# Five plain pairs and three seven-product pairs instead of six and two in the first pass of a retention and softplus-FFN kernel

## The chip, the cores and the metric

The kernel runs on one core of a Trainium2 chip. The metric is the device time of one execution in microseconds (us); lower is better. The core has five engines that run their own instruction streams and wait for each other through semaphores: PE (matrix products; its weight loads are shown as PEld), DVE (elementwise work), ACT (activations and copies), POOL (slower elementwise work) and SP, which here only issues DMAs.

## The reference, cut to what matters

```python
scores = scale * q @ k.T                     # per batch (8), head (8): 576 x 64
ret = scores * Dmat                          # decay gamma ** (i - j), lower triangle
x = (ret @ v).transpose(...).reshape(4608, 512)
h = x @ w_in                                 # 512 -> 2048
g = np.maximum(h, 0.0) + np.log1p(np.exp(-np.abs(h)))
return g @ w_out                             # 2048 -> 512, float32
```

A retention (attention with a decay instead of a softmax) gives 4608 tokens of 512 values; a two-layer network with a softplus between follows.

## The kernel before

All products have float32 accuracy. A value is split into a head and a rest, and a product is three matmuls (`TERMS`: rest by head, head by rest, head by head). One matmul has a 128x128 weight tile and 512 columns.

The tokens are cut into 9 units of 512. Unit 0 is computed while the weights are prepared. Units 1 and 2 form one "super unit", which this change is about; units 3 to 8 follow in three more (`full_pair`, `full_phase`). The hidden layer has 16 slices of 128, that is 8 pairs J = 0 to 7. For a pair of hidden slices and a pair of units, the 2x2 block product can be done in two ways:

- **plain** (`plain_slot`, one call for each slice p and each unit u): two block products of 6 matmuls each, so 48 matmuls for a pair over both units;
- **seven products** (`strassen_pair`, line 1022): 7 block products, 42 matmuls, and additions on DVE and ACT. It gives both units at once; the results of unit 2 are stored in `kept_dram` and fetched again at the end of the pass over unit 2 (`kept_parts`).

`PLAIN = 6` (line 56) sets how many pairs are plain. The order on all engines is the order in which the code is written: first 12 plain slots of unit 1 (p = 0 to 11), then the seven-product pairs J = 6 and 7, then 12 plain slots of unit 2, then the four kept slices of J = 6 and 7, then `full_pair`.

In a plain slot PE does the two block products into a PSUM bank (`acc` or `third`, in turn), then perhaps an attention group, then 12 output matmuls (line 504) of an earlier slice. `outputs` is a queue: slices are appended at the end of a slot and 12 matmuls are taken off in each. At the start of unit 2 the queue holds two slices of the seven-product pairs, so **in unit 2 the output matmuls of slice p run in slot p + 2**. An attention group (`chunk_products`, 13 of them in both units) is 48 to 64 small matmuls into the banks `two` and `third`; DVE then reads `third` in `states_out` (lines 272, 273, 282), masks scores (244) and scales values (430). The next product that writes `third` waits for these reads. In unit 2 the groups stand in slots with odd p, and the slot behind uses `third`.

Around this, DVE, ACT and POOL prepare things for later, by tables (`schedule`) that name a slot for each step:

- sums of blocks of the first-layer weights (`prepare_*`) and of the second-layer weights (`whole_in`, `combine_out`, `split_out`, `store_out`), stored to DRAM for the later products. `whole_in(j, at)` adds head and rest of the output weights 2j and 2j+1 (line 652) and **writes the sums into the buffers of the output weights 2at and 2at+1**, tags `w{p}`, in place of what stood there;
- combinations of the activations for units 3 and 4: `start_combined(i)` on POOL (lines 448 to 451), `finish_combined(i)` (ACT 455, DVE 456), `half_x` (ACT 435, DVE 438).

All DMAs are issued by SP, in the order written. Weight blocks come through a ring of 7 buffers, each reloaded after a product (`block_load`). `queued` is a list of DMAs that are issued one or two after each product (`queued_some`), `behind` one that is appended to `queued` later. Scratch tiles of 4 KB a partition come from a pool of 9 (`quad`).

Of the kernel before, what the change touches and what calls it, by code (L numbers as in the profile page):

```python
# [55 lines left out]
PLAIN = 6  # L56
# [28 lines left out]
def retention_softplus_ffn(ctx: ExitStack, tc, first, whole, others, consts, w, out):  # L85
# [440 lines left out]
    def output_out(u, tt, last=0):  # L526

        y = ys[u][tt]
        if u not in places:
            places[u] = [quad() for _ in range(2)]  # L530
        osb = places[u][tt // 2][:, tt % 2]
        if tt % 2 == last:
            nc.scalar.copy(osb, y)
        else:
            nc.vector.tensor_copy(osb, y)
        r = u * T + tt * P
        if u < 2:
            nc.sync.dma_start(out[r:r + P, :], osb)
        else:
            behind.append(lambda: nc.sync.dma_start(out[r:r + P, :], osb))  # L540
# [126 lines left out]
    def combine_head(f):  # L667
        for a in f:
            nc.scalar.copy(a[:, HI].bitcast(F32R), a[:, LO])
# [286 lines left out]
    def prepare_rest(j):  # L956
        combine_rest(raws[j])
# [4 lines left out]
    def raw_store(j):  # L962
        for p, n in ((2 * j, 2 * P), (2 * j + 1, 4 * P)):
            nc.sync.dma_start(wout_dram[p][:, :, 0:n].bitcast(F32), wouts[p][:, :, 0:n].bitcast(F32))
# [32 lines left out]
    def half_b22(i):  # L997
# [8 lines left out]
        (6, prepare_ring, 4, 0, 3, 2), (7, prepare_store, PLAIN + 1), (7, prepare_ring, 4, 3, 4, 3),  # L1006
        (7, finish_combined, 1, nc.vector), (7, half_b22, 2), (8, prepare_sums, 4), (9, prepare_ring, 5),
        (9, finish_combined, 2, nc.vector), (10, prepare_split, 4), (10, prepare_sums, 5), (10, half_b22, 3),
        (11, prepare_store, 4), (11, finish_combined, 3, nc.vector), (11, prepare_head, 5),
        (0, whole_out, 0), (1, combine_out, 0), (2, split_out, 0), (3, store_out, 0),  # L1010
        *[(5 + 2 * j, raw_store, j) for j in range(4)])
    starts = schedule(*[(3 + 2 * i, start_combined, i) for i in range(CPU)])
    for p in range(2 * PLAIN):
        group = groups.pop() if p % 2 == 0 and p < 10 else None
        plain_slot(1, p, B11, B21, rest, group, (), *(x.get(p, ()) for x in (jobs, starts)))
# [6 lines left out]
    def strassen_pair(s, J, group, rest, last=False, extra=None):  # L1022
# [14 lines left out]
        for j in stores:  # L1037
            prepare_rest(j)
# [27 lines left out]
        if extra is not None:  # L1066
            combine_head(raws["out", extra])
        ab4 = softplus_of(c[3])
        queued_some(len(queued))
        if group:  # L1070
            chunk_products(*group, None)
            coming_steps = next_steps(group[0]) if s == 0 and J == NJ - 1 else []
            group_out(*group)
            if extra is not None:
                combine_rest(raws["out", extra])
            for k in coming_steps:
                scale_values(k)
# [14 lines left out]
    stores = [5]  # L1092

# [6 lines left out]
    extras = {(0, NJ - 2): 1, (0, NJ - 1): 2}  # L1100
    for s in range(FULL):
# [3 lines left out]
        for J in range(first, NJ):  # L1105
            rest, kept = strassen_pair(s, J, groups.pop() if groups else None, rest, s == 0 and J == NJ - 1,
                                       extras.get((s, J)))
# [10 lines left out]
        if first:  # L1118
            blocks = schedule((0, prepare_ring, 0))
            plan = schedule(  # L1120
                *[(2 * j - 1, prepare_ring, j) for j in range(1, 4)], *[(2 * j, prepare_sums, j) for j in range(4)],
                *[(2 * j + 1, prepare_split, j) for j in range(4)], *[(2 * j + 2, prepare_store, j) for j in range(4)],
                *[(8 + 2 * i, finish_combined, i, nc.vector) for i in range(2)],
                (9, half_x, B21, STAGE[1, 0], whole, nc.vector), *[(2 * j - 7, raw_store, j) for j in range(4, NJ)],
                (4, whole_in, 3, 0), (6, combine_out, 3), (7, split_out, 3), (8, store_out, 3),
                (8, whole_in, 4, 1), (9, combine_out, 4), (10, split_out, 4), (11, store_out, 4))
            starts = schedule(*[(min(6 + 2 * i, 2 * first - 1), start_combined, i) for i in range(CPU)])
            for p in range(2 * first):
                group = groups.pop() if p % 2 else None
                if p == 0:  # L1130
                    while stores:
                        prepare_rest(stores[0])
                        prepare_store(stores.pop(0))
                if p == 2 * first - 1:
                    kept += [fetch(first)]
                plain_slot(u2, p, B12, B22, rest, group, *(x.get(p, ()) for x in (blocks, plan, starts)))
                rest = []
            job((0, 0), finish_combined, 2, nc.vector)
            job((0, 1), half_x, B11, STAGE[0, 0], whole, nc.vector)
            job((1, 0), finish_combined, 3, nc.vector)  # L1140
            job((1, 1), half_x, B22, STAGE[1, 1], whole, nc.vector)
        else:
# [5 lines left out]
        for n, J in enumerate(range(first, NJ)):  # L1148
# [5 lines left out]
            while stores:  # L1154
                prepare_rest(stores[0])
                prepare_store(stores.pop(0))
# [281 lines left out]
```

## Time and profile before

| | |
|---|---|
| three runs | 820.05, 820.60, 820.61 us; median 820.6 |
| profiled execution | 820.36 us, its span 818.6 us |
| busy time | PE 810.1 us (99%), DVE 572.4 (70%), ACT 394.7 (48%), POOL 135.4 (17%) |
| granted TensorE clock | 0.999 of full speed |
| DMA | 209.92 MB, 256 GB/s mean |
| unit 1 and the seven-product pairs | 115 to 227 us of the span |
| unit 2, plain | 227 to 303 us |
| kept slices and the first `full_pair` | 303 to 332 us |

The span runs from the first to the last instruction; 1.76 us of the profiled execution lie around it. Matmul ends are modelled in the trace, so matmuls are read by their starts.

### The profile page before, as it was taken

To read this page: it belongs to the slowest core of one execution; us is meant where nothing else is said; L and a number is where in the kernel's file an instruction comes from. 1 tells how busy PE (TensorE), PEld (TensorE's weight loads), DVE (VectorE), ACT (ScalarE), POOL (GpSimd) and SP (SyncE) were. 2 spreads that over 40 slices of the span, in tenths; PEclk is the share of its full clock that TensorE was granted. 3 is DMA by queue.
4 is the path that set the end of the run, shared out by engine and by line. 5 is a ranking of instruction groups with operands and counts; after the bars stand their busy time and mean duration, and the time that the engine had idled before them with its cause. 6 is when DMAs were issued, how large, how long until landed. Compare 5 with 4: busy or idle time off the path is not lost.

```text
span 818.6 us, 18782 instructions
## 1 busy us (share of the span) xinstructions
PE 810.1 (99%) x7369; PEld 664.9 (81%) x7369; DVE 572.4 (70%) x962; ACT 394.7 (48%) x698; POOL 135.4 (17%) x208
## 2 busy tenths in 40 slices
PE   8999999999999999999999999999999999999998
PEld 6778878888888888888888888888888888888886
DVE  5999976776676784756869984656769944345785
ACT  6778763324522434534354564334355644434543
POOL 4322221541121453112111000111100000000000
PEclk9999999999999999999999999999999999999999
DMA  9998879887889985698888778778757676666665
GB/s 360 322 314 288 314 241 370 292 293 254 283 307 346 329 281 171 200 318 261 276 260 298 219 222 253 255 234 262 221 170 222 216 242 199 194 195 192 201 212 172
DMA packets 149399, 209.92 MB, mean 256 GB/s; under 512 B 10816, under 2 KB 115008, under 8 KB 149312
## 3 DMA queue, kind: packets, MB, share of 16 engines
q1 hardware_dynamic: 149312, 208.72, 77.4%
q8 instruction: 59, 0.97, 0.5%
q14 instruction: 28, 0.23, 0.1%
HBM read 166.74 MB, written 41.94 MB: 255 GB/s over the span
## 4 chain that ended last, share of the span: by engine, by line
PE 97%; DMA 1%; DVE 0%; SPq 0%; issue 0%; ACT 0%; DVEq 0%
PE acc L891 21%; PE sum L1183 20%; PE y L504 16%; PE third L891 12%; PE h L465 5%; PE two L891 5%; PE two L1183 4%; PE third L226 2%; PE third L1183 2%; PE acc L1183 2%; PE two L210 2%; PE two L288 2%; PE two L300 1%; DMA raw<-whole 1%; PE bank L210 0%
## 5 line engine op out<-in xcount | busy, mean ns | idle before, releaser
L891 PE MATMUL acc<-xt,ring 128*128 128x512 f32 x768 | 193.3, 389 | 0.1
L1183 PE MATMUL sum<-parts,ring 128*128 128x512 f32 (+1 forms) x723 | 173.7, 391 | 0.0
L891 PEld LDWEIGHTS acc<-xt,ring 128*128 128x128 f32 x768 | 143.9, 188 | 30.8 <-DVE quad L1056 0.5
L1183 PEld LDWEIGHTS sum<-parts,ring 128*128 128x128 f32 x723 | 134.2, 188 | 28.2
L1177 DVE TENSOR_TENSOR parts<-g,parts 128x512 fp32r<-128x512 f32 x168 | 113.5, 692 | 52.8 <-ACT parts L1173 51.7
L504 PE MATMUL y<-wout,g 128*128 128x512 f32 x576 | 141.0, 393 | 0.0
L1173 ACT CAST parts<-g 128x512 fp32r<-128x512 f32 x168 | 103.8, 622 | 68.5 <-PE sum L1183 25.3
L504 PEld LDWEIGHTS y<-wout,g 128*128 128x128 f32 x576 | 106.6, 188 | 24.2 <-DVE g L497 1.7
L891 PE MATMUL third<-xt,ring 128*128 128x512 f32 x444 | 110.9, 389 | 0.0
L891 PEld LDWEIGHTS third<-xt,ring 128*128 128x128 f32 x444 | 83.4, 188 | 17.3
L488 ACT ACTIVATE g<-g 128x512 f32<-128x512 f32 x96 | 59.0, 631 | 78.4 <-DVE g L1205 36.2
L203 POOL TENSOR_TENSOR qv<-qv,consts_sb 128x256 f32<-128x256 f32 x61 | 43.0, 705 | 132.8 <-DMA qv<-others 129.3
L1205 DVE TENSOR_TENSOR g<-two,g 128x512 f32<-128x512 f32 x24 | 16.6, 692 | 54.2 <-PE two L891 51.8
L497 DVE TENSOR_TENSOR g<-ab,g 128x512 fp32r<-128x512 f32 x44 | 31.6, 718 | 27.4 <-ACT g L493 26.7
L465 PE MATMUL h<-xt,win 128*128 128x512 f32 x192 | 47.8, 397 | 1.5 <-ACT xt L414 1.5
L493 ACT CAST g<-ab 128x512 fp32r<-128x512 f32 x44 | 27.3, 621 | 44.5 <-PE y L504 40.6
L1203 ACT COPY g<-acc 128x512 f32<-128x512 f32 x24 | 14.1, 588 | 68.7 <-PE acc L891 68.7
L465 PEld LDWEIGHTS h<-xt,win 128*128 128x128 f32 x192 | 35.1, 188 | 10.0 <-ACT xt L414 2.2
L891 PE MATMUL two<-xt,ring 128*128 128x512 f32 x168 | 42.6, 390 | 0.0
L284 POOL TENSOR_TENSOR s<-s,consts_sb 128x256 f32<-128x256 f32 (+1 forms) x31 | 20.7, 667 | 106.7 <-DVE s L282 95.7
L891 PEld LDWEIGHTS two<-xt,ring 128*128 128x128 f32 x168 | 31.4, 188 | 6.8 <-DVE xs L430 0.3
L226 PEld LDWEIGHTS third<-qv,keys 64*64 64x64 f32 x776 | 27.0, 134 | 9.0 <-issue 8.6
(186 smaller groups left out, 1199.7 us busy)
## 6 DMA issues: line engine op xcount, KB each, us to landing
ring<-split SPq DMA_DIRECT2D x126, 256.0 KB, 4.5
ring<-combined SPq DMA_DIRECT2D x104, 256.0 KB, 3.6
ring<-outcombined SPq DMA_DIRECT2D x96, 256.0 KB, 3.4
qv<-others SPq DMA_DIRECT2D x61, 320.0 KB, 4.7
ring<-outsplit SPq DMA_DIRECT2D x72, 256.0 KB, 3.5
wst<-w SPq DMA_DIRECT2D x32, 512.0 KB, 5.8
keys<-others SPq DMA_DIRECT2D x61, 256.0 KB, 4.9
split<-win SPq DMA_DIRECT2D x16, 512.0 KB, 6.0
```

Of the source, the lines that this page charges most:

```text
L203: nc.gpsimd.tensor_mul(v, v, f.unsqueeze(2).broadcast_to([P, 4, D]))
L226: return nc.tensor.matmul(L["T"][rows[h], t, part[s]], L["kp"][rows[t], s, rows[h]], L["v"][rows[t], s, rows[h]], start=True, stop=True, s ...
L284: nc.gpsimd.tensor_mul(s, s, f.unsqueeze(2).broadcast_to([P, 2 * n, D]))
L465: nc.tensor.matmul(h, wins[p][:, a, kt * P:(kt + 1) * P], xt[:, b, T1 + kt // 2, kt % 2], start=(n == 0), stop=(n == 3 * NKT - 1))
L488: nc.scalar.activation(out, h, AF.Softplus)
L493: nc.scalar.copy(g[:, HI], ab)
L497: nc.vector.tensor_sub(g[:, LO], ab, g[:, HI].bitcast(F32))
L504: nc.tensor.matmul(ys[u][tt], g[:, a, tt * P:(tt + 1) * P], wouts[p][:, b], start=(p == 0 and n == 0), stop=(p == NF - 1 and n == 2))
L891: nc.tensor.matmul(bank, w[:, ta, kt * P:(kt + 1) * P], xt[:, tb, x, kt], start=start and k == 0, stop=k == 5, skip_group_check=True)
L1173: nc.scalar.copy(t[:, HI], g_slot(J, n))
L1177: nc.vector.tensor_sub(t[:, LO], g_slot(J, n), t[:, HI].bitcast(F32))
L1183: nc.tensor.matmul(bank[m][:, at], w[:, a, m * P:(m + 1) * P], t[:, b, at], start=start and n == 0, stop=n == 2, skip_group_check=True)
```

## The change

`PLAIN` becomes 5: unit 1 has 10 plain slots, then the seven-product pairs J = 5, 6, 7, then 10 plain slots of unit 2 and six kept slices. The number of attention groups stays 13: five in the plain slots of unit 1, three (before: two) in seven-product pairs, five (before: six) in unit 2. The tables are rewritten for the shorter passes. The first-layer sums of pair 7 are now made inside the seven-product pair J = 5, for use in J = 7. The stores of unit 0's and 1's outputs and of the second-layer weights go through `queued`.

```diff
-PLAIN = 6
+PLAIN = 5
@@ output_out
-        if u < 2:
-            nc.sync.dma_start(out[r:r + P, :], osb)
-        else:
-            behind.append(lambda: nc.sync.dma_start(out[r:r + P, :], osb))
+        (queued if u < 2 else behind).append(lambda: nc.sync.dma_start(out[r:r + P, :], osb))
@@ raw_store
-            nc.sync.dma_start(wout_dram[p][:, :, 0:n].bitcast(F32), wouts[p][:, :, 0:n].bitcast(F32))
+            queued.append(lambda p=p, n=n: nc.sync.dma_start(wout_dram[p][:, :, 0:n].bitcast(F32),
+                                                             wouts[p][:, :, 0:n].bitcast(F32)))
@@ unit 1's slots
-        group = groups.pop() if p % 2 == 0 and p < 10 else None
+        group = groups.pop() if p % 2 == 0 else None
@@ strassen_pair
-    def strassen_pair(s, J, group, rest, last=False, extra=None):
+    def strassen_pair(s, J, group, rest, last=False, extra=None, more=None):
...
-        for j in stores:
-            prepare_rest(j)
+        if more is not None:
+            prepare_whole(more)
+            prepare_sums(more)
...
+        if more is not None:
+            prepare_head(more)
+            if more + 1 < NJ:
+                prepare(more + 1)
...
+            if more is not None:
+                prepare_rest(more)
+                stores.append(more)
...
+    late_sums = {PLAIN: PLAIN + 2}
@@ unit 2's table, the rows of the second-layer sums
-                (4, whole_in, 3, 0), (6, combine_out, 3), (7, split_out, 3), (8, store_out, 3),
-                (8, whole_in, 4, 1), (9, combine_out, 4), (10, split_out, 4), (11, store_out, 4))
-            starts = schedule(*[(min(6 + 2 * i, 2 * first - 1), start_combined, i) for i in range(CPU)])
+                (2, whole_in, 3, 0), (4, combine_out, 3), (6, split_out, 3), (7, store_out, 3), (8, whole_in, 4, 3))
+            starts = schedule(*[(min(4 + 2 * i, 2 * first - 1), start_combined, i) for i in range(CPU)])
```

Three places show what moves. Names: `wout3_182` is output weight 3 and so on, `sums_` the tile that `whole_in` writes (its first tile takes the first buffer named by `at`, its second tile the second), `u`, `sx`, `s` what `states_out` makes, `y0` to `y3` the four output banks.

DVE in unit 2, around `whole_in(3, 0)`. Before, it stands in slot 4:

```order
L497 TENSOR_TENSOR g_3399<-ab_3397,g_3399 128x512
L662 TENSOR_TENSOR quad_3369<-quad_3370 128x256
L663 TENSOR_TENSOR quad_3369<-quad_3369 128x256
L664 TENSOR_TENSOR quad_3370<-quad_3369 128x256
L665 TENSOR_TENSOR quad_3370<-quad_3369,quad_3370 128x256
L652 TENSOR_TENSOR sums_3420<-wout6_185 128x512
L652 TENSOR_TENSOR sums_3421<-wout7_972 128x512
L272 TENSOR_TENSOR u_3509<-third_1738,s_3346 128x256
L273 TENSOR_TENSOR sx_3508<-third_1738,s_3346 64x256
```

Now, in slot 2:

```order
L497 TENSOR_TENSOR g_3328<-ab_3326,g_3328 128x512
L659 TENSOR_TENSOR quad_3298<-quad_3299 128x256
L660 TENSOR_TENSOR quad_3298<-quad_3298 128x256
L661 TENSOR_TENSOR quad_3299<-quad_3298 128x256
L662 TENSOR_TENSOR quad_3299<-quad_3298,quad_3299 128x256
L649 TENSOR_TENSOR sums_3353<-wout6_185 128x512
L649 TENSOR_TENSOR sums_3354<-wout7_972 128x512
L272 TENSOR_TENSOR u_3444<-third_1738,s_3269 128x256
L273 TENSOR_TENSOR sx_3443<-third_1738,s_3269 64x256
```

The rows read alike, two slots earlier: the two additions write the buffers of output weights 0 and 1, and behind them stand the state steps of the next slot's group.

PE right behind that group. Before (slot 5):

```order
L300 MATMUL two_1736<-qv_3154,sx_3341 64x64
L504 MATMUL y0_3227<-wout3_182,g_3349 128x512 x3
L504 MATMUL y1_3228<-wout3_182,g_3349 128x512 x3
L504 MATMUL y2_3229<-wout3_182,g_3349 128x512 x3
L504 MATMUL y3_3230<-wout3_182,g_3349 128x512 x3
L891 MATMUL third_1738<-xt_186,ring_3220 128x512 x6
L891 MATMUL third_1738<-xt_186,ring_3255 128x512 x6
```

Now (slot 3):

```order
L300 MATMUL two_1736<-qv_3101,sx_3264 64x64
L504 MATMUL y0_3331<-wout1_180,g_3272 128x512 x3
L504 MATMUL y1_3332<-wout1_180,g_3272 128x512 x3
L504 MATMUL y2_3333<-wout1_180,g_3272 128x512 x3
L504 MATMUL y3_3334<-wout1_180,g_3272 128x512 x3
L888 MATMUL third_1738<-xt_186,ring_3149 128x512 x6
L888 MATMUL third_1738<-xt_186,ring_3178 128x512 x6
```

The output matmuls between the group and the next product into `third` now read output weight 1; before, that weight's last reader stood a slot ahead of `whole_in(3, 0)`.

DVE around the last group of unit 2, where `whole_in(4, .)` stands. Before, in slot 8, the sums go to the buffers of weights 2 and 3; now, also in slot 8, to those of weights 6 and 7, and slot 9 is the last. Now:

```order
L456 TENSOR_TENSOR xt_186<-quad_3706,xt_186 128x8x128
L649 TENSOR_TENSOR sums_3880<-wout8_973 128x512
L649 TENSOR_TENSOR sums_3881<-wout9_974 128x512
L272 TENSOR_TENSOR u_3984<-third_1738,s_3802 128x256
L273 TENSOR_TENSOR sx_3983<-third_1738,s_3802 64x256
L282 TENSOR_TENSOR s_3988<-third_1738,u_3984 128x256
L244 TENSOR_TENSOR a_3993<-two_1736,mask_106 128x512
L430 TENSOR_TENSOR xs_595<-two_1736,consts_sb_105 128x4x128
L497 TENSOR_TENSOR g_3991<-ab_3907,g_3991 128x512
```

PE behind the same group, now:

```order
L504 MATMUL y3_3334<-wout7_972,g_3805 128x512 x3
L504 MATMUL y0_3331<-wout8_973,g_3857 128x512 x3
L504 MATMUL y1_3332<-wout8_973,g_3857 128x512 x3
L504 MATMUL y2_3333<-wout8_973,g_3857 128x512 x3
L504 MATMUL y3_3334<-wout8_973,g_3857 128x512 x3
L504 MATMUL y0_3331<-wout9_974,g_3991 128x512 x3
```

Output weight 7 is read behind the group and ahead of weight 8; the rest `g_3991` that DVE makes last in its rows is what weight 9's matmuls read.

## Rows read from the trace of the kernel before

**Rows 1.** The page: engines, and the chain that ended last

```profile
PE 810.1 (99%) x7369; PEld 664.9 (81%) x7369; DVE 572.4 (70%) x962; ACT 394.7 (48%) x698; POOL 135.4 (17%) x208
PE 97%; DMA 1%; DVE 0%; SPq 0%; issue 0%; ACT 0%; DVEq 0%
```

**Rows 2.** Busy time by stretch (us, count), clock, DMA share, GB/s

```profile
114.92:226.60 111.68, 111.50 (x1172) 91.68 (x1171) 75.14 (x129) 44.57 (x79) 31.65 (x43) 1.00 0.87 299
226.60:302.67 76.07, 76.07 (x1014) 63.07 (x1013) 57.60 (x102) 25.64 (x47) 26.30 (x33) 1.00 0.92 322
302.67:331.67 29.00, 28.93 (x131) 23.45 (x127) 14.67 (x21) 11.35 (x18) 8.07 (x8) 1.00 0.48 156
```

**Rows 3.** The chain in order of time (start, us, what), first seven-product pair

```profile
191.96 2.72 PE y L504 x12
...
202.84 1.37 PE acc L891 x6
...
204.24 0.70 DVE quad L1056
```

**Rows 4.** Timeline of PE (start, us with the last matmul's modelled end)

```profile
204.04 0.84 PE L504 MATMUL y<-wout,g 128*128 128x512 f32 x3
204.99 1.66 PE L891 MATMUL acc<-xt,ring 128*128 128x512 f32 x6
...
221.63 1.52 PE L891 MATMUL acc<-xt,ring 128*128 128x512 f32 x6
```

**Rows 5.** Timeline of PE around the group of unit 2's slot 5

```profile
263.26 3.02 PE L504 MATMUL y<-wout,g 128*128 128x512 f32 x12
266.12 2.20 PE L891 MATMUL third<-xt,ring 128*128 128x512 f32 x9
```

**Rows 6.** Timeline of DVE around the same group

```profile
261.96 1.29 DVE L652 TENSOR_TENSOR sums<-wout 128x512 f32<-128x512 f32 x2
263.17 0.42 DVE L272 TENSOR_TENSOR u<-third,s 128x256 f32<-128x256 f32 x1
263.61 0.42 DVE L273 TENSOR_TENSOR sx<-third,s 64x256 f32<-64x256 f32 x1
```

**Rows 7.** Timeline of DVE in a seven-product pair

```profile
197.51 0.69 DVE L1032 TENSOR_TENSOR quad<-two,quad 128x512 f32<-128x512 f32 x1 [2.05 <-PE two L891]
198.12 1.28 DVE L652 TENSOR_TENSOR quad<-wout 128x512 f32<-128x512 f32 x2
```

**Rows 8.** Timeline of DVE, the last group of unit 2 and the kept slices

```profile
294.24 1.22 DVE L438 TENSOR_TENSOR xt<-xs,xt 128x1024 fp32r<-128x1024 f32 x1 [0.26 <-ACT xt L435]
...
302.94 0.42 DVE L272 TENSOR_TENSOR u<-third,s 128x256 f32<-128x256 f32 x1
...
304.79 0.68 DVE L430 TENSOR_TENSOR xs<-two,consts_sb 128x512 f32<-128x512 f32 x1
306.43 0.69 DVE L497 TENSOR_TENSOR g<-ab,g 128x512 fp32r<-128x512 f32 x1 [0.96 <-ACT g L493]
...
312.77 1.43 DVE L438 TENSOR_TENSOR xt<-xs,xt 128x1024 fp32r<-128x1024 f32 x1 [0.26 <-ACT xt L435]
...
318.19 0.69 DVE L497 TENSOR_TENSOR g<-quad,g 128x512 fp32r<-128x512 f32 x1
```

**Rows 9.** Timeline of PE, the kept slices and what follows

```profile
302.67 13.90 PE L504 MATMUL y<-wout,g 128*128 128x512 f32 x60
316.40 1.52 PE L891 MATMUL acc<-xt,ring 128*128 128x512 f32 x6
```

**Rows 10.** Timeline of POOL behind the last group

```profile
309.41 0.86 POOL L203 TENSOR_TENSOR qv<-qv,consts_sb 128x256 f32<-128x256 f32 x1 [1.26 <-DMA qv<-others]
310.22 1.72 POOL L448 TENSOR_TENSOR quad<-xs 128x256 f32<-128x256 f32 x1
```

**Rows 11.** Line 448 in all: min/median/max ns

```profile
L448 POOL TENSOR_TENSOR quad<-xs x8: 733/834/1723, 144.1 to 310.2; 128x256 f32<-128x256 f32 x8
```

**Rows 12.** The longest total waits (waiter <- awaited: us, times, longest)

```profile
POOL qv L203 <- DMA qv<-others: 129.3, 57, 7.3
```

More of the change, by code (lines that the diff above doesn't have):

```diff
@@ L1005, in retention_softplus_ffn @@
         (5, finish_combined, 0, nc.vector), (5, half_b22, 1), (6, prepare_split, PLAIN + 1),
[L1006 to L1009, printed above, removed]
+        (7, prepare_store, PLAIN + 1), (7, finish_combined, 1, nc.vector), (7, half_b22, 2), (8, prepare, PLAIN + 2),
+        (9, finish_combined, 2, nc.vector), (9, half_b22, 3), (9, finish_combined, 3, nc.vector),
         (0, whole_out, 0), (1, combine_out, 0), (2, split_out, 0), (3, store_out, 0),
-        *[(5 + 2 * j, raw_store, j) for j in range(4)])
-    starts = schedule(*[(3 + 2 * i, start_combined, i) for i in range(CPU)])
+        *[(5 + 2 * j, raw_store, j) for j in range(3)])
+    starts = schedule(*[(3 + 2 * i, start_combined, i) for i in range(3)], (8, start_combined, 3, nc.vector))
     for p in range(2 * PLAIN):
-        group = groups.pop() if p % 2 == 0 and p < 10 else None
+        group = groups.pop() if p % 2 == 0 else None
         plain_slot(1, p, B11, B21, rest, group, (), *(x.get(p, ()) for x in (jobs, starts)))
@@ L1090, in strassen_pair @@
         return [split_last, lambda: softplus_rest(gs[u1, 2 * J + 1], ab4)], kept
-    stores = [5]
     def kept_parts(u, J, g, n):
@@ L1098, in kept_parts @@
         outputs_of(u, 2 * J + n)
-    extras = {(0, NJ - 2): 1, (0, NJ - 1): 2}
+    stores = []
+    extras = {NJ - 2: 1, NJ - 1: 2}
+    late_sums = {PLAIN: PLAIN + 2}
     for s in range(FULL):
@@ L1106, in retention_softplus_ffn @@
             rest, kept = strassen_pair(s, J, groups.pop() if groups else None, rest, s == 0 and J == NJ - 1,
-                                       extras.get((s, J)))
+                                       extras.get(J), late_sums.get(J))
         for f in rest:
@@ L1120, in retention_softplus_ffn @@
             plan = schedule(
[L1121 to L1124, printed above, removed]
-                (4, whole_in, 3, 0), (6, combine_out, 3), (7, split_out, 3), (8, store_out, 3),
-                (8, whole_in, 4, 1), (9, combine_out, 4), (10, split_out, 4), (11, store_out, 4))
-            starts = schedule(*[(min(6 + 2 * i, 2 * first - 1), start_combined, i) for i in range(CPU)])
+                *[(2 * j - 1, prepare_ring, j) for j in range(1, first)],
+                *[(2 * j, prepare_sums, j) for j in range(first)], *[(2 * j + 1, prepare_split, j) for j in range(first)],
+                *[(2 * j + 2, prepare_store, j) for j in range(first - 1)],
+                (6, finish_combined, 0, nc.vector), (8, finish_combined, 1, nc.vector),
+                (9, half_x, B21, STAGE[1, 0], whole, nc.vector),
+                *[(2 * j - 7, raw_store, j) for j in range(4, NJ)], (4, raw_store, 3),
+                (2, whole_in, 3, 0), (4, combine_out, 3), (6, split_out, 3), (7, store_out, 3), (8, whole_in, 4, 3))
+            starts = schedule(*[(min(4 + 2 * i, 2 * first - 1), start_combined, i) for i in range(CPU)])
             for p in range(2 * first):
                 group = groups.pop() if p % 2 else None
[L1130 to L1133, printed above, removed]
                 if p == 2 * first - 1:
@@ L1137, in retention_softplus_ffn @@
                 rest = []
+            job((0, 0), prepare_store, first - 1)
             job((0, 0), finish_combined, 2, nc.vector)
@@ L1141, in retention_softplus_ffn @@
             job((1, 1), half_x, B22, STAGE[1, 1], whole, nc.vector)
+            job((2, 0), combine_out, 4)
+            job((2, 1), split_out, 4)
+            job((2, 1), store_out, 4)
         else:
@@ L1153, in retention_softplus_ffn @@
                 f()
-            while stores:
-                prepare_rest(stores[0])
-                prepare_store(stores.pop(0))
             kept_parts(u2, J, kept[n], 1)
```

## Prediction, made before the changed kernel was run

> **What bounds the kernel now.** First the page: PE is busy 99% of the span and 97% of the chain that ended last is PE [rows 1]. Then the stretches that the change touches: in unit 2 PE is busy for all of 76.07 us, and between 115 and 332 us hardly anything is missing; the clock is granted in full, 2.4 GHz [rows 2]. So PE's matmuls set the time, and an edit counts only if it takes matmuls away or makes PE wait. Third, the chain in order of time: 12 matmuls take 2.72 us, 0.2267 each [rows 3]. Fourth, PE's one wait in these stretches, in the first seven-product pair: PE could have issued again 3 x 0.2267 us after 204.04, at 204.72, but starts at 204.99, because DVE has to add the bank first (204.24, 0.70 us) [rows 3, 4]. That is 0.27 us; and the six matmuls behind it take 1.66 instead of 1.52 us [rows 4], so **a wait of PE costs 0.14 us on top**. DMA is busy at 0.92 in unit 2, at 322 GB/s [rows 2], which makes about 350 GB/s for a full queue (322/0.92, an estimate).
>
> **What goes.** Pair 5 has 42 matmuls instead of 48. All outputs and groups stay. 6 x 0.2267 = **-1.36 us**. A group moves from unit 2 into pair J = 5; the same small matmuls run, at nothing. The first seven-product pair is now J = 5; like J = 6 before it has four output blocks of 3 left, of which one covers the wait for DVE, so the 0.27 + 0.14 us stay.
>
> **What costs nothing.** The additions for pair 7's weights in J = 5 (two like line 652's, 1.28 us for two, and four of 0.42) take the place of `whole_out` and `prepare_rest`, about as much work, and the DVE wait of 2.05 us in such a pair [rows 7] covers them. Output and raw stores were issued in line, ahead of ring loads; no ring load is late in this trace (of the first stretch's 111.68 us PE lacks 0.18 [rows 2], and the only wait there is the one above), so queueing them can gain nothing there. If the ring's lead were gone, a late load would cost what it is late.
>
> **Term A: `whole_in(3, 0)` in slot 2.** Its second addition writes over output weight 1. Output matmuls run two slots behind, so weight 1's are those of slot 3, behind that slot's group (the order of PE above). DVE must therefore wait for the end of these 12 matmuls, with the state steps of the group (272, 273) behind the addition in its stream; and the next product needs `third`, which those steps read. Before, the two additions ran without a wait in front, and 273 ended at 264.03, 2.09 us ahead of the product at 266.12 [rows 5, 6]. Now PE ends its output block and has nothing: DVE starts 0.20 us after PE's last issue slot (204.04 to 204.24 [rows 3, 4]); one addition takes 0.605 us (261.96 to 263.17 is two), 272 and 273 another 0.86 (263.17 to 264.03) [rows 6]; PE starts 0.05 us after DVE's end (204.94 to 204.99 [rows 3, 4]). Sum 1.72, with the 0.14 behind a wait **+1.86 us**. Bounds 1.5 (the two steps and the addition alone) and 2.4 (an operation stretched while POOL works, as line 438's 1.43 us against 1.22 [rows 8], and more); I take the rows' value, since nothing else is due there.
>
> Does DVE really hold what stands behind? In rows 7 it sits idle for 2.05 us in front of 1032 and then runs the sums of line 652, which need only weights and scratch, without a gap. It did not take them first. The Trainium skill, "TensorE: Matmul & The Clock Gate" (Architectural detail), says that DVE and ACT are strict first-in first-out and only PE pulls weight loads ahead. By that rule the trace agrees, and A stands; without it A and B would vanish and the sum would be the saving alone.
>
> **Term B: `whole_in(4, 3)` in slot 8.** Its second addition writes over weight 7, read in slot 9 behind the last group. Behind it on DVE stand 272, 273, 282, 244, 430 and then 497, which makes the rest that weight 9's outputs read. PE has weight 8's 12 matmuls, 2.72 us, as cover. DVE: 0.20 + 0.605 + 2.45 (302.94 to 430's end less its overlap, 305.39 [rows 8]) + 0.69 for 497 + 0.05 = 4.0 us. 4.0 - 2.72 + 0.14 = **+1.42 us**. Bounds 1.0 and 1.9 (the same stretching).
>
> **Term B'.** The next rest (weight 10's) has two rest operations (1.21), a `half_x` (1.22 to 1.43 [rows 8]) and its own 0.69 in front: 3.0 to 3.4 us after the last, against 2.72 + 0.14 of PE. **+0.3 us**, bounds 0 and 0.8.
>
> **Term C: the kept slices.** Six kept slices now follow instead of four, and `finish_combined(3)` moves from between the rests of the last two (weights 14 and 15) to between those of weights 12 and 13. Before, its chain (query and value load, POOL's scaling, four POOL operations, ACT, DVE) let the 497 behind it end at 318.88, 16.2 us after the group's end at 302.67; PE didn't care, since products started at 316.40 in between [rows 8, 9]. Now that rest is weight 13's, and PE wants it after six blocks: 6 x 2.72 + 0.23 (a first block behind a group, 302.67 to 316.40 is 5 x 2.72 + 0.13) + B + B' = about 18.2 us. With the same chain there are 2 us to spare. But SP's list in front of those loads now has two stores and a fetch of 512 KB each closer together: 1.5 MB at 350 GB/s is 4.3 us at most, 0 at least; I take 2.5, and get 16.2 + 2.5 - 18.2 + 0.14 = **+0.6 us**, bounds 0 and 2.4. POOL waits up to 7.3 us for such loads already [rows 12].
>
> POOL's line 448 takes between 733 and 1723 ns, and it was 1.72 us in this very chain [rows 10, 11]. The Trainium skill, "SBUF — State Buffer" (SBUF: two separate sides), says that POOL and a DVE operation with two SBUF inputs exclude each other on a shared port pair. The trace agrees in the spread. By that rule the chain keeps its length among DVE's many such operations; without the exclusion the chain would be short, C would be 0 and the sum 0.6 us lower.
>
> **The sum.** -1.36 + 1.86 + 1.42 + 0.3 + 0.6 = +2.8 us. On the profiled execution 820.36 + 2.8 = 823.2 us; the median of the runs shown is 0.24 us above that execution, so 823.4 us.
>
> **Rivals.**
> 1. *The saving alone.* The two additions find their buffers free, because the outputs of weights 1 and 7 are done or because DVE passes the waiting addition. Price: 820.6 - 1.36 = 819.2 us, which is no slower than before. It decides where 273 would end ahead of the output block, as it did before by 2.09 us. For it: the trace of before has no such wait anywhere. Against: two slots' lag of the outputs, which the order shows. If pair J = 5 also lost the 0.41 us wait, 818.8 us. Chance 0.11, of which 0.03 for the last.
> 2. *A stands and B is covered* (POOL and ACT late anyway, or 497 ready otherwise): -1.36 + 1.86 + 0.3, 821.4 us; likewise B without A. Chance 0.09.
> 3. *The loads come late.* The denser SP list delays query and value loads by 4 us or more, weight 13 and the products behind wait for POOL's chain: C is 2.4 to 4, 825.2 to 827 us. For it: DMA share 0.92 and POOL's waits. Against: PE waits in A and B, which lets the queue drain. Chance 0.15.
>
> **How the numbers follow.** The forecast (A, B, and C below 2.4) has 0.65: 822.0 to 825.2 us, likeliest 823.4. The range for 8 in 10 is 821.6 to 825.9 us: it takes in rival 2 in part and most of rival 3, and leaves out rival 1. About 0.2% (1.64 us: below 818.96, above 822.24) is what a measurement of this kernel can tell from no change. Slower: nearly all of the forecast and rival 3, 0.78. Same: rival 1 without its last part, rival 2, a little of the forecast, 0.18. Faster: 0.04.
>
> **What would show it.** A: PE idle some 1.7 us in unit 2 behind the output matmuls of weight 1, with DVE's line 649 waiting for PE line 504 and PE for DVE 273. B: 1.3 us ahead of weight 9's outputs, released by DVE 497. C: a wait ahead of weight 13's, released by DVE 497 behind 456, with POOL 448 to 451 in front. The first seven-product pair keeps its 0.27 us, and from the second `full_pair` on the stretches last as long as before. No wait of DVE at 649 would make the prediction wrong, and so would a late ring load in the seven-product pairs.

## Result: 0.9% slower, with waits of PE in six places

The changed kernel takes 828.0 us (median of four runs, 827.1 to 828.4) against 820.6 us before: ratio 1.0089, 95% interval 1.0072 to 1.0107. The direction was forecast, the size was not: +7.4 us instead of +2.8, outside the range. The profiled execution took 827.13 us, 6.77 more than that of before.

The page of after, engines and the chain that ended last (before: [rows 1]):

```profile
PE 810.4 (98%) x7363; PEld 663.9 (80%) x7363; DVE 574.2 (70%) x967; ACT 397.2 (48%) x701; POOL 133.8 (16%) x205
PE 95%; DVE 2%; DMA 1%; issue 1%; ACT 0%; SPq 0%; DVEq 0%; ACTq 0%
```

PE has six matmuls fewer, as counted, and its share of the chain fell from 97 to 95%. By stretch (unit 1 and the seven-product pairs; unit 2; kept slices and the first `full_pair` up to its group), with the columns of [rows 2]:

```profile
114.86:233.64 118.78, 118.11 (x1318) 97.08 (x1317) 73.47 (x129) 47.01 (x83) 31.69 (x44) 1.00 0.87 295
233.64:300.22 66.58, 63.49 (x837) 52.01 (x837) 51.30 (x94) 21.06 (x39) 22.41 (x29) 1.00 0.92 328
300.22:337.16 36.94, 35.21 (x156) 27.77 (x150) 25.01 (x34) 15.64 (x24) 8.96 (x8) 1.00 0.53 198
```

In unit 2 PE was busy for all of 76.07 us before. Now it lacks 3.1 of 66.58, and 1.7 of the 36.94 behind. The clock is granted in full throughout. What PE waited for between 180 and 345 us (engine and line, awaited, us in total, times, longest):

```profile
PE y L504 <- DVE g L497: 1.7, 2, 1.0
PE third L888 <- ACT quad L666: 1.6, 1, 1.6
PE third L888 <- DVE s L282: 1.5, 1, 1.5
PE two L300 <- issue: 1.3, 1, 1.3
PE third L226 <- issue: 0.5, 1, 0.5
```

Measured from one start of a matmul to the next, and with the longer second matmul behind each wait (0.07 to 0.14 us), the account is this:

| where (us of the span) | what | on record | measured |
|---|---|---|---|
| pair 5 | six matmuls fewer | -1.36 | -1.36 |
| 212, group of J = 6 | keys land late | none | +0.71 |
| 260, third product of slot 4 | term A | +1.86 | +1.87 |
| 288, third product of slot 8 | splits ahead of the state steps | none | +1.79 |
| 306 | term B, rest of weight 9 | +1.42 | +1.26 |
| 310 | term B', rest of weight 10 | +0.3 | +1.01 |
| 319, weight 13's outputs | term C | +0.6 | 0 |
| 303 to 322 | pieces of under 0.1 us in the kept slices | none | +0.36 |
| 339, first group of `full_pair` | wait with no semaphore | none | +1.66 |

To the first product of `full_pair` the terms make 5.64 us, and that product moved from 316.40 [rows 9] to 322.04. With the last line it is 7.30; 0.5 us of it is given back behind, 0.3 of that behind PE's last matmul, where the change touches nothing, and I didn't follow it further.

### The profile page after: what moved, and what is told of

Its sections match the earlier page's. It is cut to its first block, busy times and chain, and to the rows that moved or that the text cites. A ratio compares the mean times of both kernels' runs of the same rounds, so it can differ in the third digit from the quotient of the medians.

```text
span 825.4 us, 18783 instructions
## 1 busy us (share of the span) xinstructions
PE 810.4 (98%) x7363; PEld 663.9 (80%) x7363; DVE 574.2 (70%) x967; ACT 397.2 (48%) x701; POOL 133.8 (16%) x205
## 4 chain that ended last, share of the span: by engine, by line
PE 95%; DVE 2%; DMA 1%; issue 1%; ACT 0%; SPq 0%; DVEq 0%; ACTq 0%
PE acc L888 21%; PE sum L1185 20%; PE y L504 15%; PE third L888 12%; PE h L465 5%; PE two L888 5%; PE two L1185 4%; PE third L226 2%; PE third L1185 2%; PE acc L1185 2%; PE two L288 2%; PE two L210 2%; PE two L300 1%; DMA raw<-whole 1%; PE pair L360 0%
## 5 line engine op out<-in xcount | busy, mean ns | idle before, releaser
L888 PE MATMUL third<-xt,ring 128*128 128x512 f32 x432 | 108.4, 390 | 3.1 <-ACT quad L666 1.6
L888 PEld LDWEIGHTS third<-xt,ring 128*128 128x128 f32 x432 | 81.0, 188 | 20.6 <-ACT quad L666 2.0
L203 POOL TENSOR_TENSOR qv<-qv,consts_sb 128x256 f32<-128x256 f32 x61 | 47.4, 778 | 140.2 <-DMA qv<-others 139.0
L244 DVE TENSOR_TENSOR a<-two,mask 128x512 f32<-128x512 f32 (+1 forms) x28 | 19.0, 677 | 23.1 <-PE third L226 16.2
```

Of the source, the lines that this page charges most:

```text
L203: nc.gpsimd.tensor_mul(v, v, f.unsqueeze(2).broadcast_to([P, 4, D]))
L244: nc.vector.tensor_mul(a.rearrange("p h s c -> p (h s) c"), live[steps[0]]["S all"].rearrange("p h (s c) -> p h s c", c=HC), mask.unsqueez ...
L888: nc.tensor.matmul(bank, w[:, ta, kt * P:(kt + 1) * P], xt[:, tb, x, kt], start=start and k == 0, stop=k == 5, skip_group_check=True)
```

## Six readings in the trace of after

**Term A** came as foreseen. Timeline of DVE, and PE's two rows around (start, us, what, [idle before <- releaser]):

```profile
255.43 0.68 DVE L649 TENSOR_TENSOR sums<-wout 128x512 f32<-128x512 f32 x1
260.21 0.69 DVE L649 TENSOR_TENSOR sums<-wout 128x512 f32<-128x512 f32 x1 [4.10 <-PE y L504]
260.82 0.41 DVE L272 TENSOR_TENSOR u<-third,s 128x256 f32<-128x256 f32 x1
261.25 0.42 DVE L273 TENSOR_TENSOR sx<-third,s 64x256 f32<-64x256 f32 x1
...
257.15 3.02 PE L504 MATMUL y<-wout,g 128*128 128x512 f32 x12
261.77 1.16 PE L888 MATMUL third<-xt,ring 128*128 128x512 f32 x4 [1.59 <-ACT quad L666]
```

The second addition waits 4.10 us for the output matmuls of weight 1 ([rows 6]: before, the two additions ran without a wait), the two state steps queue behind it, and PE starts 0.10 us after 273's end (261.25 + 0.42). The profile names ACT's 666 as releaser; that copy ended at 261.40, so by the times it was DVE.

**The wait in slot 8** isn't in the prediction. Ahead of the state steps of slot 7's group stand, in DVE's stream, slot 6's sums (659 to 662) and, new in this slot, `finish_combined(0)` (456, before in slot 8) and `split_out(3)` (670, before in slot 7). Timeline of DVE, a row of POOL, a row of PE:

```profile
281.37 0.69 DVE L497 TENSOR_TENSOR g<-ab,g 128x512 fp32r<-128x512 f32 x1 [2.22 <-ACT g L493]
281.98 0.42 DVE L659 TENSOR_TENSOR quad<-quad 128x256 f32<-128x256 f32 x1
...
283.95 0.95 DVE L662 TENSOR_TENSOR quad<-quad 128x256 f32<-128x256 f32 x1
284.82 1.74 DVE L456 TENSOR_TENSOR xt<-quad,xt 128x1024 fp32r<-128x1024 f32 x1
286.49 2.02 DVE L670 TENSOR_TENSOR sums<-sums 128x512 fp32r<-128x512 f32 x2
...
289.32 0.42 DVE L282 TENSOR_TENSOR s<-third,u 128x256 f32<-128x256 f32 x1
...
285.45 1.71 POOL L451 TENSOR_TENSOR quad<-xs,quad 128x256 f32<-128x256 f32 x1
...
289.81 0.96 PE L888 MATMUL third<-xt,ring 128*128 128x512 f32 x3 [1.49 <-DVE s L282]
```

DVE has no gap from 281.37 on, and its operations are long: 0.95 us for a 128x256 addition that takes 0.42 elsewhere, 2.02 for a pair that takes 1.28. In the same time POOL runs the four operations of `start_combined(1)`, 282.83 to 287.16.

**Terms B and B'.** DVE, then PE:

```profile
303.28 0.69 DVE L649 TENSOR_TENSOR sums<-wout 128x512 f32<-128x512 f32 x1 [1.59 <-PE y L504]
...
306.32 0.68 DVE L497 TENSOR_TENSOR g<-ab,g 128x512 fp32r<-128x512 f32 x1
306.92 1.70 DVE L670 TENSOR_TENSOR quad<-quad 128x512 fp32r<-128x512 f32 x2
308.55 1.21 DVE L438 TENSOR_TENSOR xt<-xs,xt 128x1024 fp32r<-128x1024 f32 x1
309.68 1.10 DVE L497 TENSOR_TENSOR g<-quad,g 128x512 fp32r<-128x512 f32 x1
...
307.06 3.04 PE L504 MATMUL y<-wout,g 128*128 128x512 f32 x12 [0.98 <-DVE g L497]
310.83 11.37 PE L504 MATMUL y<-wout,g 128*128 128x512 f32 x48 [0.74 <-DVE g L497]
```

B is nearly what was worked out. B' is three times as long, because the two splits took 1.70 us instead of 1.28 and the rest 1.10 instead of 0.69, again with POOL at work.

**Term C** cost nothing here. The rest of weight 13 is made behind its chain:

```profile
318.14 0.68 DVE L497 TENSOR_TENSOR g<-quad,g 128x512 fp32r<-128x512 f32 x1
```

It ends at 318.82, 18.6 us after the group's end at 300.22, as the prediction had it (16.2 + 2.5). But PE, held up in B and B', comes to weight 13 only at 319.32, the fourth of the four slices in its last row, and doesn't wait. The 0.36 us in the table lie in front of it and aren't C's.

**The late keys.** SP's timeline, and below it its longest wait between 195 and 216 us (columns as in the list of PE's waits):

```profile
202.68 0.86 SPq L678 DMA_DIRECT2D combined<-quad  x2
208.91 0.52 SPq L620 DMA_DIRECT2D ring<-combined  x1
209.48 0.59 SPq L162 DMA_DIRECT2D keys<-others  x1
```

```profile
SPq L620 <- DMA combined<-quad: 5.3, 1, 5.3
```

The sums of pair 7 are now stored inside J = 6, just ahead of the ring load that reads them back. SP stands 5.3 us until the stores have landed; the group's keys are issued behind, at 209.48, and land 3.6 us later, at 213.1. PE's group stops for 0.49 us at 212.66 and goes on at 213.15.

**The wait with no semaphore.** In the first group of units 3 and 4 PE stands still, and its row of the timeline names no releaser:

```profile
340.65 0.27 PE L300 MATMUL two<-qv,s 64*64 64x64 f32 x1 [1.29 <-issue]
```

The DMA view of after from the group's start (337.23) to the wait's end has a row of instruction loads (queue, packets, MB, share):

```profile
q8 instruction: 1, 0.02, 2.2%
```

Between 309.5 and 337.23 that view has no row of instruction loads at all. In before, one falls between 305 and the group's start at 331.67, and the group has no wait. That this queue brings PE's code fits the counts: the page of after has 59 loads on it, and PE has 15149 instructions in the trace, 257 for each load.

```profile
q8 instruction: 59, 0.97, 0.4%
```

The group has 128 small matmuls (in units 1 and 2 groups have 56 to 128, not the 48 to 64 given at the start), with their weight loads 256 instructions in some 2 us.

## Experiments

All medians stand beside 820.3 to 820.9 us of the kernel before in the same runs. Runs of one kernel with such waits scatter by 1 to 5 us, and the interval of each single edit overlaps that of the change (1.0072 to 1.0107), so for single edits the trace decides more than the median.

**One wait taken away at a time.**

```diff
-(2, whole_in, 3, 0), (4, combine_out, 3),
+(4, whole_in, 3, 0), (5, combine_out, 3),
```

> The changed kernel with whole_in(3, 0) in slot 4 (as before the change) instead of slot 2, and combine_out(3) in slot 5; split_out and all else stay. The second addition then finds output weight 1 read. Theory (five separate stalls, each with its own cause): only the wait at the third product of slot 4 goes, 1.87 us of the trace; 827.98 - 1.87 = 826.1 us (825.7 to 826.5), and the wait of about 1.8 us in slot 8 stays. Rival (DVE has too much to do in unit 2 whatever stands where; a stall taken away comes back one group later): 827.5 us or more, and the wait in slot 6 or 8 grows. Second rival (the stalls are one chain, and the one in slot 8 follows from the first): both go, 824.3 us.

825.7 us, ratio 1.0062 (1.0050 to 1.0075). The wait in slot 4 is gone from the trace, the one in slot 8 is there with 1.2 us (expected about 1.8). A stands, and the waits aren't one chain.

```diff
-(6, split_out, 3), (7, store_out, 3)
+(7, split_out, 3), (8, store_out, 3)
```

> The changed kernel with split_out(3) in slot 7 instead of 6 and store_out(3) in 8 instead of 7. The two ACT copies and the two DVE subtractions (2.02 us in the trace) then no longer stand in front of the state steps of slot 7's group. Theory (DVE's work ahead of those steps, stretched while POOL works, ends 1.65 us too late for slot 8's product): the wait in slot 8 goes, 827.98 - 1.79 = 826.2 us (825.8 to 826.6). Rival (the two subtractions delay slot 8's own work as much, so the wait moves to slot 9 and the outputs behind it): 827.5 us or more, with the waits at the outputs of weights 9 and 10 grown by 1 us or more.

826.8 us, ratio 1.0072 (1.0059 to 1.0086), 0.2 above the expected range. PE's waits from 180 to 345 us are now these two, of which the second is term A's:

```profile
PE y L504 <- DVE g L497: 1.9, 3, 0.8
PE third L888 <- ACT quad L666: 1.6, 1, 1.6
```

The wait in slot 8 is gone; those at the outputs of weights 9 and 10 are smaller than in after (1.00 and 0.48 us from start to start, and another of 0.24), and one of 0.92 us appears at 318.5 in the kept slices.

```diff
-(8, whole_in, 4, 3)
+(8, whole_in, 4, 1)
```

> The changed kernel with whole_in(4, 1) in slot 8, as before the change: the sums of weights 8 and 9 go to the buffers of output weights 2 and 3, which are long read. Theory: DVE no longer waits 1.59 us for the outputs of weight 7, the rest of weight 9 is ready in time, and the first wait at the outputs goes (1.15 + 0.11 us); the second (0.90 + 0.11 us, weight 10's rest behind operations stretched while POOL works) shrinks, since DVE is 1.6 us ahead: 827.98 - 2.3 = 825.7 us (825.4 to 826.8). Rival (DVE's queue is full to the end of unit 2 anyway, the wait only hid in it): less than 0.5 us, 827.5 us or more.

825.8 us, ratio 1.0064 (1.0050 to 1.0078). Both waits at the outputs are gone, and one of 0.70 us appears at 318.7.

```diff
+        while stores:
+            prepare_store(stores.pop(0))
         c = [q[:, n] for q in (quad(), quad()) for n in range(2)]
...
-        while stores:
-            prepare_store(stores.pop(0))
         product(z, T1, True)
```

> The changed kernel with the two stores of pair 7's sums issued at the start of the seven-product pair J = 6 instead of behind its second product, about 4 us earlier. Theory (SP stands 5.7 us at the ring load that reads these stores back, and the keys of the group in J = 6 are issued behind it and land 0.7 us late): the group's wait of 0.71 us goes; 827.98 - 0.7 = 827.3 us (827.0 to 827.6). Rival (the stores wait for DVE's rests at the start of the pair and hold ring loads behind them): 828.0 us or more, with a wait at a product of J = 6. Second rival (the DMA queues are late for the keys whatever stands in front): no change, 828.0 us.

826.8 us, ratio 1.0079 (1.0067 to 1.0092). SP's wait for the stores is gone, and so is the group's. Some luck is in it: of the seven traces of five-pair kernels with the stores in their old place the group waited some 0.3 to 0.9 us in four, of the seven with the stores moved in none.

**Is it POOL that makes DVE long?** `start_combined(1)` one slot later, all of DVE's work where it was:

```diff
-            starts = schedule(*[(min(4 + 2 * i, 2 * first - 1), start_combined, i) for i in range(CPU)])
+            starts = schedule((4, start_combined, 0), (7, start_combined, 1), (8, start_combined, 2), (9, start_combined, 3))
```

> The changed kernel with POOL's start_combined(1) in slot 7 instead of 6 (the others stay in 4, 8 and 9): DVE's work is where it was, but POOL's four operations no longer run while DVE does slot 6's sums, subtractions and split. In the trace of after these DVE operations took 281.98 to 288.51 with POOL at work; at the durations that the same lines have without POOL (line 659 to 662 1.6 us, 456 1.14, 670 1.2 for two) they would end 2.5 us sooner. Theory (the wait of 1.65 us in slot 8 is made by the stretching): the wait in slot 8 goes or falls below 0.3 us, 826.2 us (825.7 to 827.0). Rival (the number of DVE operations makes it, POOL does not matter): the wait stays above 1.2 us, 827.5 us or more. The operations of start_combined(1) now run against slot 8's DVE work, so the waits at the outputs of weights 9 and 10 may grow by up to 1 us.

The same place on DVE, without POOL:

```profile
282.00 0.41 DVE L659 TENSOR_TENSOR quad<-quad 128x256 f32<-128x256 f32 x1
...
283.24 0.42 DVE L662 TENSOR_TENSOR quad<-quad 128x256 f32<-128x256 f32 x1
283.58 1.22 DVE L456 TENSOR_TENSOR xt<-quad,xt 128x1024 fp32r<-128x1024 f32 x1
284.71 1.49 DVE L670 TENSOR_TENSOR sums<-sums 128x512 fp32r<-128x512 f32 x2
286.13 0.41 DVE L272 TENSOR_TENSOR u<-third,s 128x256 f32<-128x256 f32 x1
```

The state steps begin 4.1 us after 659 instead of 6.5, and the wait in slot 8 is gone. It is also gone with the split in slot 7 and POOL at work as before, so the wait needs both, the split and the stretching. The Trainium skill, "SBUF — State Buffer" (SBUF: two separate sides), has POOL and a DVE operation with two SBUF inputs exclude each other; with 0.42 against up to 0.96 us for one addition the traces agree. The kernel as a whole isn't better, 828.7 us (ratio 1.0102, 1.0083 to 1.0120), above the expected range and the rival's bound: `start_combined(1)` now waits behind the value scalings of the next group until 294.70, and the `finish_combined` behind it holds ACT's stream for 4.28 us, so that PE's next group waits 2.3 us for a copy of ACT. I had looked only at DVE's side.

**The queueing alone**, on the kernel before.

```diff
-            nc.sync.dma_start(wout_dram[p][:, :, 0:n].bitcast(F32), wouts[p][:, :, 0:n].bitcast(F32))
+            queued.append(lambda p=p, n=n: nc.sync.dma_start(wout_dram[p][:, :, 0:n].bitcast(F32),
+                                                             wouts[p][:, :, 0:n].bitcast(F32)))
```

(and the same for the outputs of units 0 and 1.)

> The kernel before with one part of the change alone: output and second-layer weight stores of the first units go through the queue of DMAs instead of being issued in line. Theory (no ring load was late, so there is nothing to gain or lose): same as before within 0.3 us. Rival (the stores now delay group loads or make SP wait for buffers): slower by 0.7 us or more, with a wait of PE in the seven-product pairs.

821.2 us, ratio 1.0011 (1.0003 to 1.0020). So it isn't free; it costs some 0.2 to 1.6 us. The trace has two new waits, 0.5 us at 101.2 (PE for POOL's scaling of values) and 0.3 at 280.4 (PE for DVE), none in the seven-product pairs where the rival had it; that the queueing makes them isn't shown.

**All four edits together.**

> The changed kernel with four edits together: whole_in(3, 0) in slot 4 and combine_out(3) in 5, split_out(3) in 7 and store_out(3) in 8, whole_in(4, 1) in slot 8, and the stores of pair 7's sums at the start of the pair J = 6. Theory (separate stalls that add): 827.98 - 1.87 - 1.79 - 2.27 - 0.71 = 821.3 us; with a wait in the kept slices that only shows when the earlier ones are gone (0.70 and 0.92 us where one of them was taken away) 822.1 us (820.8 to 822.8). Rival (the same DVE work makes new waits): 823.5 us or more.

823.3 us, ratio 1.0031 (1.0019 to 1.0043), half a microsecond above the expected range. The trace has 1.48 us at 315.9, from start to start, in place of the 0.7 to 0.9 expected. It stands ahead of weight 13's outputs: **term C**, uncovered by the other edits. POOL, ACT and DVE in its chain:

```profile
312.18 0.73 POOL L451 TENSOR_TENSOR quad<-xs,quad 128x256 f32<-128x256 f32 x1
...
312.94 1.05 ACT L455 CAST xt<-quad 128x1024 fp32r<-128x1024 f32 x1 [3.06 <-POOL quad L451]
...
314.02 1.23 DVE L456 TENSOR_TENSOR xt<-quad,xt 128x1024 fp32r<-128x1024 f32 x1 [3.10 <-ACT xt L455]
```

With that step two kept slices later:

```diff
-            job((1, 0), finish_combined, 3, nc.vector)
-            job((1, 1), half_x, B22, STAGE[1, 1], whole, nc.vector)
-            job((2, 0), combine_out, 4)
+            job((1, 0), half_x, B22, STAGE[1, 1], whole, nc.vector)
+            job((2, 0), finish_combined, 3, nc.vector)
+            job((2, 1), combine_out, 4)
```

> As the kernel with the four edits, and finish_combined(3) two kept slices later, behind half_x(B22) (term C of the prediction: the chain through POOL then no longer stands between the rests of weights 12 and 13). Theory: the wait of 0.7 to 0.9 us in the kept slices goes, 821.3 us where the group of the first pair of units 3 and 4 waits without a semaphore (1.0 to 1.7 us in four of five traces), 819.9 where it does not. Rival (finish_combined(3) is then late for the third product of that pair): a wait at that product, 822.1 us or more.

825.3 us, ratio 1.0056 (1.0043 to 1.0069), worse. The wait at 315.9 is gone, but `combine_out(4)` and `split_out(4)` now stand in one slot. ACT's copies of the second wait for DVE's sums of the first, the product's copy (1205) waits behind them in ACT's stream, and PE waits 2.0 us for it, at 319.4 to 321.4. Neither theory had this. Busy time by stretch, columns as in [rows 2], from that wait on:

```profile
317.00:321.40 4.40, 2.44 (x12) 1.70 (x10) 3.25 (x7) 1.99 (x4) 0.00 (x0) 1.00 0.00 0
321.40:325.80 4.40, 4.40 (x12) 3.50 (x13) 0.86 (x2) 1.22 (x2) 0.00 (x0) 0.61 0.88 319
```

Behind it the granted clock is 0.61, mostly its lower level of 1.2 GHz: the next six matmuls take 2.62 us instead of 1.36.

**The combinations on DVE.** The four edits, with POOL's four operations as DVE's:

```diff
-            starts = schedule(*[(min(4 + 2 * i, 2 * first - 1), start_combined, i) for i in range(CPU)])
+            starts = schedule(*[(4 + 2 * i, start_combined, i, nc.vector) for i in range(3)])
...
-            job((1, 0), finish_combined, 3, nc.vector)
-            job((1, 1), half_x, B22, STAGE[1, 1], whole, nc.vector)
+            job((0, 1), start_combined, 3, nc.vector)
+            job((1, 0), half_x, B22, STAGE[1, 1], whole, nc.vector)
+            job((1, 1), finish_combined, 3, nc.vector)
```

> As the kernel with the four edits (823.3 us), and the four combinations of unit 2 (start_combined, lines 448 to 451) on DVE instead of POOL; the last of them stands in the second kept slice, and finish_combined(3) one kept slice later. POOL then only scales values in this stretch. DVE gets 4 x 4 x 0.42 us more to do (that is what a 128x256 addition takes it), but its own operations are no longer stretched (by 0.5 to 2.5 us for each of POOL's four operations in the traces so far), and ACT 455 no longer waits for POOL behind the late value loads. Theory: no DVE operation above its usual time in slots 6 to 9, and the waits of 0.3 + 0.5 + 1.5 us go: 821.0 us (820.3 to 821.8) with the group's wait without a semaphore, 819.6 without. Rival (DVE is the bound of unit 2, and 6.7 us more of it make waits in slots 6 or 8): 823.5 us or more.

821.2 us, ratio 1.0000 (0.9991 to 1.0009), as expected. In slot 6 the four sums take their 0.41 to 0.42 us and POOL's former additions 0.41 to 0.50, as DVE's timeline shows in part:

```profile
281.00 0.42 DVE L662 TENSOR_TENSOR quad<-quad 128x256 f32<-128x256 f32 x1
281.34 1.22 DVE L456 TENSOR_TENSOR xt<-quad,xt 128x1024 fp32r<-128x1024 f32 x1
282.47 0.41 DVE L448 TENSOR_TENSOR quad<-xs 128x256 f32<-128x256 f32 x1
```

Of the longer waits PE has only one left between 115 and 345 us:

```profile
PE two L300 <- issue: 1.5, 1, 1.5
```

**The wait with no semaphore.** PE's instructions counted in the order of the trace from 0 (matmuls, weight loads, semaphore instructions), it ends each time at number 7361, 242 behind the group's first matmul. Filling matmuls at the start shift everything behind:

```diff
-FILLS = 22
+FILLS = 50
```

> The changed kernel with the 50 filling matmuls alone. Theory (code): the wait of 1.3 us in the first group of units 3 and 4 goes, all others stay: 826.7 us (826.2 to 827.3). Rival (the group itself): 828.0 us, with that wait.

829.2 us, ratio 1.0098 (1.0082 to 1.0114). The profiled run of 826.0 us has the other waits, but for that of J = 6, and not this one; the median didn't fall.

> As the kernel with the combinations on DVE, with 50 instead of 22 filling matmuls at the very start, where PE waits for the first loads. They compute nothing and only shift PE's later instructions by 112 places in its code. Theory (the wait without a semaphore in the first group of units 3 and 4 is for PE's own code: in the traces it ends each time at the same instruction, 242 behind the group's first, 1.2 to 2.6 us after a 16 KB instruction load): that instruction now stands 112 earlier against the loads, so no wait there, 1.0 to 1.7 us less than the kernel without the shift. Rival (the wait belongs to the group itself, by a semaphore that the trace does not show): it stays at the same matmul, and the two kernels are equal within 0.4 us.

821.3 us, ratio 1.0005 (0.9996 to 1.0014): no wait there either, and no gain. The first hidden product begins 1.1 and 2.2 us later in these two traces than in their neighbours; I can't tell how much of that is the shift, since it varies by up to 1.8 us without it. With `FILLS = 26`, 16 places:

> The changed kernel with 26 instead of 22 filling matmuls at the very start: a shift of PE's later instructions by only 16 places, at under 0.1 us of PE time in the opening. Theory (code: the stretch of 256 instructions that the group runs into begins 14 instructions ahead of the group, so it is used up inside the group before the next load is there): with 30 instructions ahead, some 2 us more, the next load comes in time; the wait of 1.3 us in the first group of units 3 and 4 goes and all others stay, 826.7 us (826.0 to 827.3). Rival (chance, or the group itself): the wait is there, 828.0 us.

826.7 us, ratio 1.0073 (1.0059 to 1.0087), as the theory says, and no wait there; but the interval overlaps the change's own, so the gain isn't clear of noise.

> The kernel with the four edits and the combinations on DVE (821.2 us, its profile with a single wait of 1.5 us in the first group of units 3 and 4), with 26 filling matmuls. Theory (code): no wait is left but the 0.27 us of the first seven-product pair; 821.2 - 1.4 = 819.8 us (819.0 to 820.3), 0.8 under the kernel before. Rival: the wait stays, 821.2 us, as before the shift.

820.6 us, ratio 1.0001 (0.9989 to 1.0013), 0.3 above the expected range.

> The same with the stores of units 0 and 1 and of the second-layer weights issued in line, as before the change. Theory (in the kernel before the queueing alone cost 0.1%, interval 0.03 to 0.2): 0.6 us less than its neighbour, 819.2 us (818.4 to 819.9), faster than the kernel before by 0.1 to 0.2%. Rival (the queueing costs nothing where the pairs are five): equal within 0.3 us.

820.1 us, ratio 0.9987 (0.9978 to 0.9996): **the fastest version**, 0.04 to 0.22% ahead of the kernel before, 0.2 us above the expected range. The interval overlaps its neighbour's, so what the queueing costs here isn't shown. What PE waited for from 115 us on, first in the kernel with the queue, then in that with stores in line:

```profile
PE y L504 <- issue: 1.3, 1, 1.3
PE sum L1186 <- issue: 0.9, 1, 0.9
```

```profile
PE sum L1188 <- issue: 0.6, 1, 0.6
PE y L504 <- DVE g L497: 0.3, 1, 0.3
```

The first group of units 3 and 4 is clean, but the same wait stands elsewhere, and the places fit: it ends at numbers 6849 and 12225 (the latter in both kernels), which are 512 before and 4864 behind 7361, that is 2 x 256 and 19 x 256. By its places the wait is tied to every 256th instruction of PE. In eight of nine traces with five plain pairs and no shift it stood in the first group of units 3 and 4, in none of the five with a shift. The Trainium skill, "Runtime: NRT & Kernel Launch" (Instruction fetch mechanics), says that an engine's code comes in blocks of 16 KiB, 256 instructions, and the traces agree in the distance. It also calls the crossing from one block to the next mostly hidden; here it isn't always, with 0.6 to 1.7 us of standing still. That a group which runs through 256 instructions in 2 us outruns the load of the next block fits this, but is argued. What decides in each run when the load goes out stays open: in the one unshifted trace without the wait it went out before the group. And no median shows what the wait costs: with shifts the kernels took 829.2, 826.7, 821.3 and 820.6 us, against 828.0 and 821.2 without.

## Why the prediction was right in direction and wrong in size

- **What bounds the kernel, the saving, the wait that stays.** Right. PE sets the time, 1.36 us were saved, and the first seven-product pair keeps its wait (264 ns too long from start to start, before 266).
- **Term A.** Right to 0.01 us, in place and mechanism; the edit that undoes it removes the wait.
- **Term B.** Right in mechanism, 0.16 us too high.
- **Term B'.** The term was mis-sized: 1.01 us for 0.3, above its upper bound of 0.8. The prediction had allowed for stretching ([rows 8], 1.43 against 1.22) in the `half_x` only; that one came out at 1.21, and the splits and the rest were stretched, by 0.83 us together.
- **Term C.** The chain came out as long as forecast, 18.6 us. Wrong was that it adds to B and B': while PE waits there, C's chain has time. It cost nothing instead of 0.6 us, and 1.48 when the other waits were gone.
- **"What costs nothing".** This step failed. It looked at the seven-product pairs and not at unit 2's own table, where `split_out(3)` went from slot 7, behind that slot's state steps, and `finish_combined(0)` from slot 8 to slot 6, beside the sums, all in front of slot 7's state steps, and with POOL at work: 1.79 us. The same reasoning that gave A and B (DVE in order, state steps behind, the next product waiting) would have found it, had each slot of the table been added up with POOL's operations beside it.
- **"No ring load is late, so queueing can gain nothing".** The queue was taken as free; alone, in the kernel before, it costs about 0.1%. And the stores of pair 7's sums, moved into J = 6, were weighed for DVE and not for SP, which must wait for them to land: 0.71 us.
- **The wait with no semaphore**, 1.66 us, couldn't be read from the trace of before. It was not in the bounds.
- **Rivals.** None of the three happened. The third (late query and value loads) named late DMAs, but in the kept slices; what was late were the keys of J = 6.

On the profiled executions the sum was 4.0 us short (6.8 against 2.8): 1.79 + 0.71 + 1.66 = 4.16 are in three places that it doesn't have, 0.7 in B', -0.8 in B and C, 0.4 in small pieces, and -0.5 behind the changed part. That it isn't further off is luck: -0.8 and -0.5 stand against the rest.

## What to carry to other kernels

Where a table moves work between slots, add up each engine's stream slot by slot up to the step that the next product needs, and do it for the loads and stores of the DMA queue as well; one wait that is found is a reason to look for more in the same stream. POOL's help can cost the engine that it helps more than the work it takes over: in slot 6 four additions of POOL stretched DVE's work by 2.3 us (6.5 against 4.1), and DVE did the four itself in 1.6. With all sixteen on DVE, and one step a slice later, the kernel became 2.1 us faster; by the traces the largest part, 1.5 us, is C's wait, whose chain no longer goes through POOL. A wait that is taken away uncovers the next, so single edits don't add up.

## What the runs showed of the hardware

- A 128x256 addition on DVE takes 0.42 us alone and 0.72 to 0.96 beside POOL's additions; POOL's own take 0.72 to 1.72 us, and the same additions 0.41 to 0.62 on DVE.
- Behind one wait of 2.0 us in the kernel with `finish_combined(3)` moved, and behind two, of 2.3 and 2.0 us, in that with `start_combined(1)` moved, PE ran at its lower clock, 0.43 us for a matmul, for 7 or 8 matmuls; in after, with waits of 0.5 to 1.6 us, the granted clock stayed at 1.00.
- PE can stand still for 0.6 to 1.7 us without a semaphore, in or just behind a run of small matmuls; the places where it did lie multiples of 256 of its instructions apart.
- A store to DRAM that is read back at once held SP for 5.3 us.
